# LN ahead of K, and Q units inside the K stage: a change of schedule in a fused attention and GEGLU kernel

## The chip, the cores and the metric

The kernel runs on one core of a Trainium2 chip. The metric is the device time of one execution in microseconds (us). Most executions of one kernel agree within a few tenths of a per cent; the widest spread of a kernel's fast runs here is 0.9%. A verdict of "faster" or "slower" needs more than 2%, and is "unclear" where the interval reaches that limit. PE is the engine of matmuls, PEld its weight loads, DVE the vector engine, ACT the scalar engine, POOL the GpSimd engine, SP the one that issues the DMAs here. The clock is the share of PE's full clock that the profile says was granted. LN is the layer norm; its last step on DVE is the normalise. K(n) and Gram(n) are the K and the Gram matmuls of tile n. PSUM is the memory that matmuls write to, in eight banks. A row-tiled pair is two Q units whose matmuls use 64 rows each and run side by side.

## The reference

All in bfloat16, S = 2048 tokens, D = 576, 32 heads of 18, F = 4608:

```python
xn  = layernorm(x)                                  # no gain, no bias
q, k, v = split(xn @ wqkv)                          # 32 heads of 18
phi = lambda t: where(t > 0, t + 1, exp(t)) + 1e-6
kv  = einsum("bhsd,bhse->bhde", phi(k), v);  z = sum_s phi(k)
o   = einsum("bhqd,bhde->bhqe", phi(q), kv) / (phi(q) . z + 1e-6)
out = x + o @ wo + (gelu(xn @ w_gate) * (xn @ w_up)) @ w_down
```

The kernel never forms V: it accumulates Gram = xn^T phi(k) over the tokens (with a column of ones for z), and kv is w_v^T Gram.

## The kernel before

The kernel writes its instructions in an order that it sorts out of planned times. Each engine works through its own instructions in that order, and semaphores hold it where an input or a buffer isn't ready. Only the first sixth of the span concerns us, up to the start of the gate/up matmuls:

- start: LN and PE transposes of tiles 0 to 3;
- K stage: for each of 16 tiles of 128 tokens LN on DVE and ACT, a crossbar transpose (a DMA) from tile 4 on, ten K matmuls, phi(k) on ACT, DVE and POOL, ten Gram matmuls;
- rest: 20 units of Q (4 chunks of 512 tokens by 5 groups of heads), the last part of Gram ("Gram B"), z and kv.

```python
def k_relu(n, hf):                     # one half of K, one PSUM bank
    if hf == 0:
        k_ea[n] = phi_tiles()          # e: 3 buffers, a: 2 buffers
    nc.scalar.activation(out=k_ea[n][0][:, hs], in_=ps_all[:, k_bank(n, hf), :HALF], func=ACT.Relu, scale=-1.0)
def k_max(n, hf):    ...               # DVE: a = max(ps, 0) + eps, same bank
def k_exp(n):        ...               # ACT: e = exp(-e)
def k_add(n):        ...               # POOL: pk = e + a
...
TILE = 2.5                             # planned us per tile
STEPS = [
    (lambda n: ln_half(n, 0), [3.02, 3.99, 6.44, 7.41, 9.44]),
    ...
    (ln_norm, [4.96, 5.69, 8.38, 10.77, 12.80]),
    (ln_dup, [5.43, 6.16, 8.85, 11.24, 13.27]),        # the transpose follows it
    ...
    (lambda n: k_half(n, 0), [6.86, 8.09, 10.30, 13.01, 15.56]),
    ...
]
...
for i in range(2, 2 * NCH):            # after the K stage: Q units 2 to 9, Gram B and copies between
    q_unit(i) ...
for k, items in enumerate([[(2, 0), (2, 1)], [(2, 2), (2, 3)], ...]):   # ten units in row-tiled pairs
    ...
```

A Q unit has one of two forms of phi. The add form is relu (ACT), max (DVE), exp (ACT), add (POOL). The min form is exp (ACT), max (DVE) and a `scalar_tensor_tensor` with min (DVE), which I call the min op.

## Time and profile before

| | before |
|---|---|
| time, median (in brackets the medians of the later rounds) | 538.54 (538.4 to 539.0) us |
| PE busy | 97% of the span of 537.7 us |
| K(4) starts | 17.21 us |
| first row-tiled Q pair starts | 75.50 us |
| gate/up starts | 85.77 us |
| stall in gate/up | 0.86 us at 91.82 |

In the table of waits, each line tells which engine and line stood still for whose result: total us, times, longest. The line that matters for the stretch from 5 to 62 us is:

```profile
PE ps_all L247 <- DMA xnT<-xn: 10.1, 9, 2.4
```

L247 is K, `xnT<-xn` the crossbar transpose. PE waits ten microseconds for transposes, and a clock that drops to half after one such wait, from 35.30 to 38.71 us, adds more. The prediction shows the other lines.

### The profile page before, as it was taken

How to read it: one execution, taken by the hardware profiler on the slowest of the kernel's cores; microseconds unless marked ns; L12 is line 12 of the kernel's file. 1: busy time of each engine (PE TensorE's matmuls, PEld its weight loads, DVE VectorE, ACT ScalarE, POOL GpSimd, SP SyncE). 2: the span in 40 equal slices, each digit the busy share in tenths (PEclk: the TensorE clock that was granted, in tenths of full speed). 3: DMA queues.
4: the chain of work that ended last, by engine and by line, in shares of the span. 5: the costliest groups of instructions: out<-in, count | busy, mean ns of one | idle time of the engine just before them, and what ended most of it. 6: DMA issues, size and time to landing. Idle time of an engine off the chain costs nothing.

```text
span 537.7 us, 10777 instructions
## 1 busy us (share of the span) xinstructions
PE 520.0 (97%) x4537; PEld 313.9 (58%) x4537; DVE 250.7 (47%) x414; ACT 143.7 (27%) x278; POOL 70.5 (13%) x85
## 2 busy tenths in 40 slices
PE   8778999999999999999999999999999999999997
PEld 7556676544457774444477754444677644445775
DVE  7745557687636813333358423333386133333100
...
PEclk9989999999999999999999999999999999999999
...
GB/s 226 154 132 154 40 1 45 237 249 271 217 131 12 12 11 166 155 152 158 146 33 24 12 121 154 155 145 159 77 11 23 78 155 153 156 134 2 12 12 23
DMA packets 106955, 57.90 MB, mean 108 GB/s; under 512 B 13402, under 2 KB 106522, under 8 KB 106906
## 3 DMA queue, kind: packets, MB, share of 16 engines
...
q14 instruction: 14, 0.11, 0.1%
...
## 4 chain that ended last, share of the span: by engine, by line
PE 86%; DMA 4%; DVE 3%; ACT 2%; POOL 1%; issue 1%; SPq 1%; DVEq 0%; ACTq 0%; POOLq 0%
PE ps_all L329 52%; PE ps_all L633 26%; PE ps_all L638 4%; DMA xnT<-xn 3%; PE ps_all L247 1%; PE ps_all L294 1%; POOL pqT L386 1%; PE ps_all L357 1%; DMA x_sb<-in_A_x_dram 1%; PE ps_all L442 1%; ACT phi_e L264 1%; DVE phi_a L384 1%; DVE phi_a L390 1%; DVE stats L210 1%; DVE phi_a L268 0%
## 5 line engine op out<-in xcount | busy, mean ns | idle before, releaser
L329 PE MATMUL ps_all<-xnT,wg 64*128 64x512 bf16 x1152 | 272.7, 376 | 0.0
L329 PE MATMUL ps_all<-xnT,wu 64*128 64x512 bf16 x1152 | 268.5, 376 | 0.0
L604 DVE TENSOR_TENSOR hT<-ps_all,gl 128x512 bf16<-128x512 f32 x144 | 99.4, 691 | 160.0 <-ACT gl L603 159.5
L603 ACT ACTIVATE gl<-ps_all 128x512 f32<-128x512 f32 x144 | 86.0, 598 | 312.5 <-PE ps_all L329 293.1
L329 PEld LDWEIGHTS <-wg 64*128 64x128 bf16 x1152 | 108.2, 94 | 68.9 <-issue 1.1
L633 PE MATMUL ps_all<-wd_sb,hT 128*128 128x288 bf16 x1152 | 147.0, 286 | 0.0
L329 PEld LDWEIGHTS <-wu 64*128 64x128 bf16 x1152 | 107.0, 94 | 67.2
L633 PEld LDWEIGHTS <-hT 128*128 128x128 bf16 x1152 | 112.3, 98 | 30.6 <-issue 1.3
L466 DVE RECIPROCAL den_sb<-den_sb 126x128 f32<-126x128 f32 (+1 forms) x80 | 68.3, 911 | 0.5
L469 POOL TENSOR_TENSOR pqT<-pqT,den_sb 126x512 bf16<-126x512 bf16 (+3 forms) x25 | 24.1, 966 | 297.7 <-DVE den_sb L466 279.1
L329 PE MATMUL ps_all<-xnT,wr 64*128 64x512 bf16 x288 | 61.9, 376 | 0.7 <-DVE phi_a L390 0.7
L641 DVE TENSOR_TENSOR res<-ps_all,x_sb 128x288 bf16<-128x288 f32 x32 | 14.6, 458 | 88.0 <-PE ps_all L638 88.0
L247 PE MATMUL ps_all<-wqkv_sb,xnT 128*128 128x288 bf16 x160 | 24.3, 296 | 10.8 <-DMA xnT<-xn 10.1
L329 PEld LDWEIGHTS <-wr 64*128 64x128 bf16 x288 | 17.1, 94 | 17.1 <-issue 0.7
L247 PEld LDWEIGHTS <-xnT 128*128 128x128 bf16 x160 | 14.9, 100 | 17.5 <-DMA xnT<-xn 12.1
L638 PE MATMUL ps_all<-m_sb,pqT 126*128 126x288 bf16 (+1 forms) x160 | 24.9, 285 | 0.0
L294 PE MATMUL ps_all<-hT,xn 128*128 128x288 bf16 (+3 forms) x192 | 23.4, 269 | 0.1
L279 POOL TENSOR_TENSOR hT<-phi_e,phi_a 128x576 bf16<-128x576 f32 x16 | 22.4, 1401 | 3.1 <-DVE phi_a L268 2.3
L268 DVE TENSOR_SCALAR phi_a<-ps_all 128x288 f32<-128x288 f32 x32 | 14.2, 450 | 17.5 <-ACT phi_e L264 15.8
L294 PEld LDWEIGHTS <-xn 128*128 128x128 bf16 (+1 forms) x192 | 18.5, 103 | 4.7 <-issue 0.6
L386 POOL TENSOR_TENSOR pqT<-phi_e,phi_a 126x512 bf16<-126x512 f32 (+1 forms) x13 | 16.3, 1267 | 21.2 <-DVE phi_a L384 17.3
L638 PEld LDWEIGHTS <-pqT 126*128 126x128 bf16 (+1 forms) x160 | 15.5, 97 | 4.1
...
## 6 DMA issues: line engine op xcount, KB each, us to landing
...
```

What stands on the lines that cost most here:

```text
L247: nc.tensor.matmul(ps_all[:, k_bank(n, hf), :HALF], lhsT=xnT[:, kt, n * P:(n + 1) * P], rhs=wqkv_sb[:, kt, D + hf * HALF:D + (hf + 1) * HALF],
L279: nc.gpsimd.tensor_tensor(out=pk[:, n, :], in0=e[:], in1=a[:], op=ALU.add)
L294: nc.tensor.matmul(ps_all[:m, b, col:col + w], lhsT=xn[:, n, j0:j0 + m], rhs=pk[:, n, d0:d0 + w], start=(n == 0 and col == 0), stop=(n == ...
L329: return nc.tensor.matmul(self.outs[i], lhsT=self.lhs(i, rows, kt), rhs=self.rhs(i, rows, kt), start=start, stop=stop, skip_group_check=True,)
L386: nc.gpsimd.tensor_tensor(out=pqT[:rows, c, cs], in0=e, in1=a, op=ALU.add)
L466: nc.vector.reciprocal(out=d[:, h:h + P], in_=d[:, h:h + P])
L469: nc.gpsimd.tensor_tensor(out=pqT[:rows, c, cols], in0=pqT[:rows, c, cols], in1=d, op=ALU.mult)
L603: nc.scalar.activation(out=gl[:], in_=ps_all[:, b[0], :], func=ACT.Gelu_apprx_tanh)
L604: nc.vector.tensor_tensor(out=hT[:, GUB * k + i, :], in0=ps_all[:, b[1], :], in1=gl[:], op=ALU.mult)
L633: nc.tensor.matmul(acc, lhsT=hT[:, f, j * P:(j + 1) * P], rhs=wd_sb[:, f, hs], start=(f == 0), stop=False,)
L638: nc.tensor.matmul(acc, lhsT=pqT[:rows, c, ts_], rhs=m_sb[:rows, c, hs], start=False, stop=(c == NCH - 1),)
L641: nc.vector.tensor_tensor(out=res[:, hs], in0=acc, in1=x_sb[:, n, hs], op=ALU.add)
```

## The change

Its intent: LN and the transpose behind it run further ahead of K (in the plan the transpose is issued 4.2 us before its K instead of 2.3), so that it has landed when K wants it, and the PE time that the K stage leaves is filled with Q. Twelve Q units go into the K stage, one per tile from tile 4 on. The last eight run as four row-tiled pairs right after it, ahead of Gram B, z and kv. K's relu and max cover both banks in one instruction from tile 4 on. The planned pace is 3.34 us per tile. The loads of w_q and of x are issued at once. The core of the diff:

```diff
+    load_w(0)
+    load_x(8, 4)
+    load_x(12, 4)
...
-        a = awork.tile([P, D], F32, name="phi_a", tag="phi_a", bufs=2)
+        a = awork.tile([P, D], F32, name="phi_a", tag="phi_a", bufs=3)
...
+        if hf is None:
+            e, a = (t[:].rearrange("p (h d) -> p h d", h=2) for t in k_ea[n])
+            return ps_all[:, k_bank(n, 0):k_bank(n, 0) + 2, :HALF], e, a
...
-    TILE = 2.5
+    TILE = 3.34
...
+        (ln_norm, [x_, 6.71, 7.42, 9.93, 11.02, 15.50, 16.52]),
+        (ln_dup, [5.86, 7.18, 7.89, 11.49, 11.73, 15.97, 18.87]),
+        (dma_transposes, [x_, x_, x_, x_, 12.02, 16.26, 19.16]),
+        (lambda n: k_half(n, 0), [6.85, 8.62, 11.23, 14.97, 16.67, 20.01, 23.33]),
...
+    Q_STEPS = [
+        (q_unit, [17.90, 21.23, 25.60, 28.93]),
+        (q_first, [19.29, 23.06, 26.80, 30.13]),
+        (q_max, [19.96, 24.03, 27.47, 30.80]),
+        (q_exp, [19.96, 23.73, 27.47, 30.80]),
+        (q_last, [21.20, 24.78, 28.22, 31.55]),
+    ]
+    NQ = 12
...
+    q_banks = _Ring([5, 6, 7, 0, 1, 2, 3, 4])
+    for k, units in enumerate([[12, 13], [15, 16], [17, 18], [14, 19], None]):
...
+    for n in range(NS):
+        g_accumulate(n, G_B)
```

More of the change, by code (lines that the diff above doesn't have):

```diff
@@ L39 @@
 NWARM = 38
-GLAG = 2
 TD = 4
@@ L148 @@
     kvT = persist.tile([P, NCH, CR], BF16, name="kvT")
+    nc.vector.memset(pqT[HP:P, NCH - 1, 0:2 * SC], 0.0)
+    nc.vector.memset(zrep[HP:P, NCH - 1, :], 0.0)
     def load_wo():
@@ L217, in ln_rstd, with ln_norm @@
         nc.scalar.activation(out=r, in_=r, func=ACT.Exp, scale=-0.5)
-    def ln_norm(n):
+    def ln_norm(n, c0=0, c1=D):
         nc.vector.tensor_scalar(
-            out=xn[:, n, 0:D], in0=x_sb[:, n, :], scalar1=mv[:, n, 0:1], scalar2=rstd[:, n:n + 1],
+            out=xn[:, n, c0:c1], in0=x_sb[:, n, c0:c1], scalar1=mv[:, n, 0:1], scalar2=rstd[:, n:n + 1],
             op0=ALU.subtract, op1=ALU.mult,
@@ L226, in ln_dup, with tp_bank, transposes, tp_copy @@
         (nc.gpsimd if n else nc.vector).tensor_copy(out=xn[:, n, D:640], in_=xn[:, n, 512:D])
-    tp_bank = ps_all[:, 7, :].bitcast(BF16).rearrange("p (k t) -> p k t", t=P)
-    def transposes(n):
-        for kt in range(KT):
-            nc.tensor.transpose(tp_bank[:, kt, :], xn[:, n, kt * P:(kt + 1) * P], ident[:])
+    vcopy, acopy = nc.vector.tensor_copy, nc.scalar.copy
+    def tp_bank(b):
+        return ps_all[:, b, :].bitcast(BF16).rearrange("p (k t) -> p k t", t=P)
+    def transposes(n, k0=0, k1=KT, b=7):
+        for kt in range(k0, k1):
+            nc.tensor.transpose(tp_bank(b)[:, kt, :], xn[:, n, kt * P:(kt + 1) * P], ident[:])
+    def tp_copy(n, k0=0, k1=KT, b=7, copy=acopy):
+        copy(out=xnT[:, k0:k1, n * P:(n + 1) * P], in_=tp_bank(b)[:, k0:k1, :])
     def dma_transposes(n):
         nc.sync.dma_start_transpose(xnT[:, :, n * P:(n + 1) * P], xn[:, n, 0:640])
-    def tp_copy(n):
-        copy = acopy if n else vcopy
-        copy(out=xnT[:, :, n * P:(n + 1) * P], in_=tp_bank[:, 0:KT, :])
     def k_bank(n, hf):
@@ L254, in phi_tiles, with k_part, k_relu, k_max @@
         e = awork.tile([P, D], F32, name="phi_e", tag="phi_e", bufs=3)
-        a = awork.tile([P, D], F32, name="phi_a", tag="phi_a", bufs=2)
+        a = awork.tile([P, D], F32, name="phi_a", tag="phi_a", bufs=3)
         return e, a
     k_ea = {}
-    def k_relu(n, hf):
-        if hf == 0:
+    def k_part(n, hf):
+        if n not in k_ea:
             k_ea[n] = phi_tiles()
+        if hf is None:
+            e, a = (t[:].rearrange("p (h d) -> p h d", h=2) for t in k_ea[n])
+            return ps_all[:, k_bank(n, 0):k_bank(n, 0) + 2, :HALF], e, a
         hs = slice(hf * HALF, (hf + 1) * HALF)
-        nc.scalar.activation(out=k_ea[n][0][:, hs], in_=ps_all[:, k_bank(n, hf), :HALF], func=ACT.Relu, scale=-1.0)
-    def k_max(n, hf):
-        hs = slice(hf * HALF, (hf + 1) * HALF)
-        nc.vector.tensor_scalar(
-            out=k_ea[n][1][:, hs], in0=ps_all[:, k_bank(n, hf), :HALF],
-            scalar1=0.0, scalar2=EPS_ATT, op0=ALU.max, op1=ALU.add,
-        )
+        return ps_all[:, k_bank(n, hf), :HALF], k_ea[n][0][:, hs], k_ea[n][1][:, hs]
+    def k_relu(n, hf=None):
+        ps, e, _ = k_part(n, hf)
+        nc.scalar.activation(out=e, in_=ps, func=ACT.Relu, scale=-1.0)
+    def k_max(n, hf=None):
+        ps, _, a = k_part(n, hf)
+        nc.vector.tensor_scalar(out=a, in0=ps, scalar1=0.0, scalar2=EPS_ATT, op0=ALU.max, op1=ALU.add)
     def k_exp(n):
@@ L278, in k_add @@
         e, a = k_ea.pop(n)
-        nc.gpsimd.tensor_tensor(out=pk[:, n, :], in0=e[:], in1=a[:], op=ALU.add)
+        (nc.gpsimd if n < NS - 1 else nc.vector).tensor_tensor(out=pk[:, n, :], in0=e[:], in1=a[:], op=ALU.add)
     G_A = {
@@ L287 @@
     }
-    G_B = {3: [(0, 0, 0, 288), (1, 0, 288, 288)]}
+    G_B = {3: [(5, 0, 0, 288), (6, 0, 288, 288)]}
     def g_accumulate(n, pieces):
@@ L297, in g_accumulate @@
                 )
-    G_B_AT = {5: range(2), 6: range(2, 9), 7: range(9, 16)}
-    vcopy, acopy = nc.vector.tensor_copy, nc.scalar.copy
     G_COPIES = {
-        4: [(0, G_A, 0, acopy), (0, G_A, 1, vcopy), (2, G_A, 0, acopy), (2, G_A, 1, vcopy)],
-        5: [(1, G_A, 0, acopy), (2, G_A, 2, vcopy)],
-        6: [(4, G_A, 2, acopy), (1, G_A, 1, vcopy)],
-        7: [(4, G_A, 0, acopy), (4, G_A, 1, vcopy), (3, G_B, 0, acopy), (3, G_B, 1, vcopy)],
-        99: [(3, G_B, 0, acopy), (3, G_B, 1, vcopy)],
+        0: [(0, 0, acopy), (2, 0, vcopy), (0, 1, acopy), (2, 1, vcopy)],
+        1: [(1, 0, acopy), (2, 2, vcopy), (4, 2, acopy), (1, 1, vcopy), (4, 0, acopy), (4, 1, vcopy)],
     }
@@ L315 @@
     SYNC = mybir.DependencyInfo(mybir.DependencyClass.Sync, mybir.DependencyReason.DATA)
-    banks = _Ring([2, 3, 4, 5, 6, 7, 0, 1])
+    banks = _Ring([3, 4, 5, 6, 7, 0, 1, 2])
     class _Unit:
@@ L349 @@
     q_banks = _Ring([7])
+    q_out, q_ea = {}, {}
+    MIN_UNITS = (2, 5, 8, 11, 13, 14, 16, 18)
     def q_unit(i):
@@ L360, in q_unit @@
             )
-        q_phi(i, sc, c, ps)
-    def q_pair(items):
-        rows = DH * HCH[items[0][1]]
-        b = [q_banks.next(), q_banks.next()]
-        outs = [ps_all[:rows, b_, :] for b_ in b]
-        def lhs(i, r, kt):
-            q0 = DH * HOFF[items[i][1]]
-            if kt == 4 and r.start:
-                return wq_lo[r, q0:q0 + rows]
-            return wqkv_sb[r, kt, q0:q0 + rows]
-        return _Unit(outs, lhs, lambda i, r, kt: xnT[r, kt, items[i][0] * SC:(items[i][0] + 1) * SC], nc.sync)
@@ L377, in q_phi, with q_pair, lhs, rhs @@
-    def q_phi(i, sc, c, ps):
-        rows = DH * HCH[c]
-        cs = slice(sc * SC, (sc + 1) * SC)
-        e, a = phi_tiles()
-        e, a = e[:rows, :SC], a[:rows, :SC]
-        if i % 3 != 2:
+        q_out[i] = ps
+    def q_pair(units):
+        rows = DH * HCH[units[0] % NCH]
+        for i in units:
+            q_out[i] = ps_all[:rows, q_banks.next(), :]
+        def lhs(a, r, kt):
+            q0 = DH * HOFF[units[a] % NCH]
+            if kt == 4 and r.start == 0:
+                return wqkv_sb[r, kt, q0:q0 + rows]
+            return (wq_lo if kt == 4 else wqkv_sb[:, kt])[r, q0:q0 + rows]
+        def rhs(a, r, kt):
+            sc = units[a] // NCH
+            return xnT[r, kt, sc * SC:(sc + 1) * SC]
+        return _Unit([q_out[i] for i in units], lhs, rhs, nc.sync)
@@ L383, in q_phi, with q_at, q_first @@
+    def q_at(i):
+        sc, c = divmod(i, NCH)
+        rows = DH * HCH[c]
+        if i not in q_ea:
+            q_ea[i] = [t[:rows, :SC] for t in phi_tiles()]
+        return (*q_ea[i], q_out[i], pqT[:rows, c, sc * SC:(sc + 1) * SC])
+    def q_first(i):
+        e, _, ps, _ = q_at(i)
+        if i not in MIN_UNITS:
             nc.scalar.activation(out=e, in_=ps, func=ACT.Relu, scale=-1.0)
-            nc.vector.tensor_scalar(out=a, in0=ps, scalar1=0.0, scalar2=EPS_ATT, op0=ALU.max, op1=ALU.add)
@@ L385, in q_phi, with q_max @@
-            nc.scalar.activation(out=e, in_=e, func=ACT.Exp, scale=-1.0)
-            nc.gpsimd.tensor_tensor(out=pqT[:rows, c, cs], in0=e, in1=a, op=ALU.add)
         else:
             nc.scalar.activation(out=e, in_=ps, func=ACT.Exp)
-            nc.vector.tensor_scalar(out=a, in0=ps, scalar1=0.0, scalar2=1.0 + EPS_ATT, op0=ALU.max, op1=ALU.add)
-            nc.vector.scalar_tensor_tensor(
-                out=pqT[:rows, c, cs], in0=e, scalar=EPS_ATT, in1=a, op0=ALU.add, op1=ALU.min)
+    def q_max(i):
+        _, a, ps, _ = q_at(i)
+        one = 0.0 if i not in MIN_UNITS else 1.0
+        nc.vector.tensor_scalar(out=a, in0=ps, scalar1=0.0, scalar2=one + EPS_ATT, op0=ALU.max, op1=ALU.add)
@@ L394, in mask_pair, with q_exp, q_last @@
+    def q_exp(i):
+        e, _, _, _ = q_at(i)
+        if i not in MIN_UNITS:
+            nc.scalar.activation(out=e, in_=e, func=ACT.Exp, scale=-1.0)
+    def q_last(i):
+        e, a, _, out_ = q_at(i)
+        if i not in MIN_UNITS:
+            nc.gpsimd.tensor_tensor(out=out_, in0=e, in1=a, op=ALU.add)
+        else:
+            nc.vector.scalar_tensor_tensor(out=out_, in0=e, scalar=EPS_ATT, in1=a, op0=ALU.add, op1=ALU.min)
     def mask_pair(dst, b4, b1):
@@ L420, in kv_stage @@
         b4, b1 = q_banks.next(), q_banks.next()
-        for c in range(NCH):
-            rows = DH * HCH[c]
-            for kt in range(KT):
+        for kt in (0, 1, 2, 4, 3):
+            for c in range(NCH):
+                rows = DH * HCH[c]
                 nc.tensor.matmul(
@@ L426, in kv_stage @@
                     rhs=g_sb[:, kt, c * CR:c * CR + rows],
-                    start=(kt == 0 and c in (0, 4)), stop=(kt == KT - 1), skip_group_check=True,
+                    start=(kt == 0 and c in (0, 4)), stop=(kt == 3), skip_group_check=True,
                 )
@@ L470, in den_norm @@
         return scale
-    TILE = 2.5
+    TILE = 3.34
+    x_ = None
     STEPS = [
-        (lambda n: ln_half(n, 0), [3.02, 3.99, 6.44, 7.41, 9.44]),
-        (lambda n: ln_half(n, 1), [3.51, 4.48, 6.93, 7.90, 9.93]),
-        (ln_rstd, [4.14, 5.11, 7.56, 10.12, 11.84]),
-        (ln_norm, [4.96, 5.69, 8.38, 10.77, 12.80]),
-        (ln_dup, [5.43, 6.16, 8.85, 11.24, 13.27]),
-        (transposes, [5.66, 6.57, 9.14, 11.53, 13.62]),
-        (tp_copy, [6.07, 6.98, 9.56, 12.27, 14.12]),
-        (lambda n: k_half(n, 0), [6.86, 8.09, 10.30, 13.01, 15.56]),
-        (lambda n: k_half(n, 1), [7.47, 9.43, 10.91, 13.91, 16.46]),
-        (lambda n: k_relu(n, 0), [7.99, 9.28, 11.56, 13.84, 16.55]),
-        (lambda n: k_relu(n, 1), [8.27, 10.55, 12.83, 15.11, 17.39]),
-        (lambda n: k_max(n, 0), [8.72, 10.41, 12.44, 14.61, 17.27]),
-        (lambda n: k_max(n, 1), [9.08, 11.11, 13.28, 15.60, 17.84]),
-        (k_exp, [8.73, 11.12, 13.29, 15.61, 18.10]),
-        (k_add, [9.59, 11.73, 14.01, 16.29, 19.88]),
-    ]
@@ L493 @@
-    SPIN = [(5.67, 7), (6.58, 2), (7.48, 3), (8.10, 2), (9.15, 3)]
-    G_AT = [11.82, 14.53, 17.07, 19.62, 22.16]
-    def at(times, n):
-        return times[n] if n < len(times) else times[-1] + TILE * (n - len(times) + 1)
-    todo = [(at(times, n), step, n) for n in range(NS) for step, times in STEPS
-            if n < TD or step not in (transposes, tp_copy)]
-    todo += [(at(STEPS[4][1], n) + 0.01, dma_transposes, n) for n in range(TD, NS)]
-    loads = [(7.0, lambda n: load_x(8, 4)), (9.5, lambda n: load_x(12, 4))]
@@ L504 @@
-    loads += [(13.5, lambda n: load_w(0)), (18.5, lambda n: load_w(2)), (23.5, lambda n: load_wo())]
-    loads += [(26.0 + 2.5 * i, lambda n, i=i: load_gu(i // 2, i % 2)) for i in range(2 * NWBUF)]
-    todo += [(t, step, 0) for t, step in loads]
-    todo += [(at(G_AT, n), lambda n: g_accumulate(n, G_A), n) for n in range(NS - GLAG)]
-    todo += [(at(STEPS[7][1], NS - 1) - 0.01, q_unit, 0), (at(G_AT, NS - GLAG) - 0.01, q_unit, 1)]
-    todo += [(at(STEPS[-1][1], 4 + n) + 0.01, lambda n: nc.gpsimd.memset(pqT[HP:P, NCH - 1, n * SC:(n + 1) * SC], 0.0), n)
-             for n in range(2)]
@@ L513 @@
-    todo += [(at(STEPS[-1][1], 7) + 0.01, lambda n: nc.gpsimd.memset(zrep[HP:P, NCH - 1, :], 0.0), 0)]
-    todo += [(t, spin, count) for t, count in SPIN]
+        (lambda n: ln_half(n, 0), [3.02, 3.99, 5.20, 7.05, 8.60, 12.08, 13.38]),
+        (lambda n: ln_half(n, 1), [3.51, 4.48, 5.96, 7.76, 9.09, 13.81, 14.53]),
+        (ln_rstd, [4.14, 6.05, 6.59, 8.44, 10.44, 14.44, 15.94]),
+        (ln_norm, [x_, 6.71, 7.42, 9.93, 11.02, 15.50, 16.52]),
+        (ln_dup, [5.86, 7.18, 7.89, 11.49, 11.73, 15.97, 18.87]),
@@ new lines @@
+        (transposes, [x_, 7.47, 9.23, 11.85]),
+        (tp_copy, [x_, 7.88, 9.88, 12.44]),
+        (dma_transposes, [x_, x_, x_, x_, 12.02, 16.26, 19.16]),
+        (lambda n: k_half(n, 0), [6.85, 8.62, 11.23, 14.97, 16.67, 20.01, 23.33]),
+        (lambda n: k_half(n, 1), [7.76, 9.52, 10.62, 13.33, 16.68, 20.02, 23.34]),
+        (lambda n: k_relu(n, 0), [7.58, 11.15, 13.00, 15.70]),
+        (lambda n: k_relu(n, 1), [8.87, 10.87, 12.16, 14.06]),
+        (k_relu, [x_, x_, x_, x_, 18.01, 21.35, 24.67]),
@@ new lines @@
+        (lambda n: k_max(n, 0), [8.24, 11.72, 13.45, 16.15]),
+        (lambda n: k_max(n, 1), [9.57, 11.36, 12.82, 14.66]),
+        (k_max, [x_, x_, x_, x_, 18.73, 22.23, 25.39]),
+        (k_exp, [9.32, 11.60, 13.45, 16.16, 18.73, 22.07, 25.39]),
+        (k_add, [10.08, 12.33, 14.18, 16.88, 19.54, 23.04, 26.20]),
+        (lambda n: g_accumulate(n, G_A), [12.14, 13.94, 15.64, 18.98, 22.31, 24.57, 27.89]),
+    ]
+    Q_STEPS = [
[5 more added lines that the diff above has]
+    ]
@@ new lines, with timed @@
+    NQ = 12
+    def timed(steps, count):
+        for step, times in steps:
+            for n in range(count):
+                last = len(times) - 1
+                if n < last or len(times) > 4 or steps is Q_STEPS:
+                    t = times[min(n, last)]
+                    if t is not None:
+                        yield t + TILE * max(n - last, 0), step, n
+                elif n == last:
+                    yield times[n], step, n
+    todo = [*timed(STEPS, NS), *timed(Q_STEPS, NQ)]
@@ new lines @@
+    todo += [
+        (4.96, lambda n: ln_norm(n, 0, 3 * P), 0), (5.57, lambda n: ln_norm(n, 3 * P, D), 0),
+        (5.33, lambda n: transposes(n, 0, 3, 7), 0), (6.09, lambda n: transposes(n, 3, KT, 4), 0),
+        (5.63, lambda n: tp_copy(n, 0, 3, 7, acopy), 0), (6.44, lambda n: tp_copy(n, 3, KT, 4, vcopy), 0),
+    ]
+    todo += [(t, spin, count) for t, count in [(5.70, 3), (6.10, 5), (7.40, 3), (8.30, 3), (9.40, 4)]]
+    loads = [lambda n: load_w(2), lambda n: load_wo()]
+    loads += [lambda n, i=i: load_gu(i // 2, i % 2) for i in range(2 * NWBUF)]
@@ L516 @@
+    todo += [(19.2 + TILE * i, step, 0) for i, step in enumerate(loads)]
     for _, step, n in sorted(todo, key=lambda x: x[0]):
@@ L523, in g_copy @@
         copy(out=g_sb[:m, kt, d0:d0 + w], in_=ps_all[:m, b, col:col + w])
-    q_banks = _Ring([5, 6, 7])
-    for i in range(2, 2 * NCH):
-        if i == 7:
-            q_banks = _Ring([2, 3, 4, 5, 6, 7])
-        q_unit(i)
-        if 3 <= i < 3 + GLAG:
-            g_accumulate(NS - GLAG + i - 3, G_A)
-        for n in G_B_AT.get(i, ()):
-            g_accumulate(n, G_B)
-        for kt, pieces, part, copy in G_COPIES.get(i, ()):
-            g_copy(kt, pieces, part, copy)
-        if i == 8:
-            z_stage()
-        if i == 8:
-            kv_stage()
-    q_banks = _Ring(list(range(8)))
+    q_banks = _Ring([5, 6, 7, 0, 1, 2, 3, 4])
     prev = None
-    for k, items in enumerate([[(2, 0), (2, 1)], [(2, 2), (2, 3)], [(2, 4), (3, 4)], [(3, 0), (3, 1)], [(3, 2), (3, 3)], None]):
-        if items:
-            u = q_pair(items)
+    for k, units in enumerate([[12, 13], [15, 16], [17, 18], [14, 19], None]):
+        if units:
+            u = q_pair(units)
             u.p1()
+        for kt, part, copy in G_COPIES.get(k, ()):
+            g_copy(kt, G_A, part, copy)
         if prev:
             prev[1].p2()
-            for i, (sc, c) in enumerate(prev[0]):
-                q_phi(2 * k + i, sc, c, prev[1].outs[i])
-        prev = (items, u)
+            for step in (q_first, q_max, q_exp, q_last):
+                for i in prev[0]:
+                    step(i)
+        prev = (units, u)
+    for n in range(NS):
+        g_accumulate(n, G_B)
+    g_copy(3, G_B, 0, acopy)
+    g_copy(3, G_B, 1, vcopy)
+    q_banks = _Ring([7, 0, 1, 2])
+    z_stage()
+    kv_stage()
     scales = []
```

## The prediction

> **What bounds the kernel now.** I read the page first: PE is busy 97% of the span, so only the stretches where it is not can give anything. The slices say where these lie: in the first sixth. I then cut that sixth into four stretches with the table of busy time by stretch (start:end, length, then busy us and instruction count of PE, PEld, DVE, ACT and POOL, clock, DMA share, GB/s).
>
> ```profile
> PE   8778999999999999999999999999999999999997
> PEclk9989999999999999999999999999999999999999
> ```
>
> ```profile
> 17.20:55.40 38.20, 28.68 (x226) 21.64 (x226) 20.31 (x59) 19.50 (x53) 19.15 (x24) 0.96 0.73 155
> 55.40:75.50 20.10, 19.95 (x148) 14.10 (x149) 11.88 (x21) 11.89 (x25) 10.29 (x8) 1.00 0.08 19
> 75.50:91.82 16.32, 15.26 (x138) 11.50 (x138) 10.72 (x19) 12.00 (x20) 8.30 (x7) 1.00 0.04 12
> ```
>
> The K stage (17.2 to 55.4) leaves PE idle for 9.5 us; Q and Gram after it and the paired Q units lose some 1.2 us. The chain of waits says why (start, length, what):
>
> ```profile
> 23.83 0.30 DVE xn L220
> ...
> 24.26 0.25 POOL xn L226
> ...
> 24.52 3.56 DMA xnT<-xn
> 28.07 0.05 issue
> 28.12 0.80 PE ps_all L247 x5
> ...
> 29.52 0.46 DVE phi_a L268
> 29.98 0.38 DVE stats L210
> ...
> 31.21 4.25 DMA xnT<-xn
> ```
>
> It is a ring: K of tile n releases a max on DVE; behind it in DVE's order stands the LN of tile n+2; its crossbar transpose takes 3.6 to 4.3 us here (2.6 where no 648 KB weight load is ahead); then K of n+2. So about 6.8 us per two tiles, while PE has only K and Gram to do. The timeline of PE shows the price and one more loss, ten K matmuls in 2.58 instead of 1.40 us after a long wait, at a granted clock of 0.50 in that half microsecond.
>
> ```profile
> 35.51 2.58 PE L247 MATMUL ps_all<-wqkv_sb,xnT 128*128 128x288 bf16 x10 [2.45 <-DMA xnT<-xn]
> 42.16 1.40 PE L247 MATMUL ps_all<-wqkv_sb,xnT 128*128 128x288 bf16 x10 [0.51 <-DMA xnT<-xn]
> 91.82 0.37 PE L329 MATMUL ps_all<-xnT,wr 64*128 64x512 bf16 x1 [0.71 <-DVE phi_a L390]
> ```
>
> Gate/up starts at 85.77 us and stalls once, 0.86 us of pace at 91.82, since the Q nonlinearities still run on DVE until 92.8. From there to the end PE is full and the change touches nothing.
>
> **What the Trainium skill says.** (1) "SBUF — State Buffer", Who interferes with whom: DVE in a 2-port mode, or with two SBUF inputs, and GpSimd take one shared port pair as an exclusive lock; who comes first keeps it for the whole instruction. The trace agrees to the hundredth: the min op of a Q unit takes 0.69 us alone and ends 0.55 after POOL's add ends when they meet.
>
> ```profile
> 61.73 1.41 POOL L279 TENSOR_TENSOR hT<-phi_e,phi_a 128x576 bf16<-128x576 f32 x1
> 62.53 1.16 DVE L391 SCALAR_TENSOR_TENSOR pqT<-phi_e,phi_a 126x512 bf16<-126x512 f32 x1
> 66.90 0.69 DVE L391 SCALAR_TENSOR_TENSOR pqT<-phi_e,phi_a 126x512 bf16<-126x512 f32 x1
> ```
>
> 62.53+1.16 = 63.69 = 63.14+0.55. The LN normalise (0.38 alone) does the same: the two met by POOL's add end 0.17 after it. (2) "PSUM — Partial Sum Buffer", PSUM bank collisions raise a hardware error: two engines must not access one bank at once, reads included. In the trace DVE's max starts 0.10 after ACT's relu of the same bank ends, always. The new relu and max over both banks therefore run one after the other. (3) "TensorE: Matmul & The Clock Gate", Back-to-back issue gap: N/2.4+2.5 ns when warm, 122.5 ns for N=288; 14 Gram matmuls start within 1.72 us, 123 ns each.
>
> **The change, part by part.** PE's work, from starts to starts: K 10 x 0.124 = 1.24; Gram A 0.98 per tile; a Q unit 1.08; a row-tiled pair 1.94 (81.08 to 83.02), 0.97 per unit. Twelve single units instead of ten cost 2 x 0.11 = 0.2 us more. Everything else of PE only moves. A tile of the K stage with a Q unit is 1.24+0.98+1.08 = 3.30 us of PE, which is why the plan has 3.34: PE is to be full, and the lead of the transpose in the plan is 23.33-19.16 = 4.2 us.
>
> Start. x(3) still lands at 8.2, x(4..7) at 9.6 (issue 4.4 plus 5.2). DVE reaches max(0,1) near 11.3 instead of 9.6 as planned; POOL's add of tile 0 stands ahead of the copy for tile 3, and the transposes of tile 3 come at 13.2 instead of 11.85. Through G(0), K(3), G(1), G(2), with the lock once, K(4) starts at about 17.9; it is 17.21 now.
>
> A steady tile, counted from the start of K(n), with durations of the trace (576 wide estimated from the 288 and 512 wide: relu 0.66, max 0.76): relu 1.50 to 2.16, max 2.26 to 3.02, POOL add 3.16 to 4.56, so Gram(n) can start at 4.64. PE wants it at 1.24+0.98+1.08+1.24 = 4.54. Balanced to 0.1 us. Then what stands in between: the normalise of n+3 is ready at 3.3, finds POOL's add holding the lock and ends at 4.73 instead of 3.7; statistics, the Q max (0.69), statistics and aggregate (0.6) follow, so max(n+1), ready at 5.56, starts at 6.2 to 6.3; in a tile whose Q unit uses the min form, after another 0.61, at 6.9. It holds both K banks: K(n+2), due at 6.60, waits for 7.0 to 7.6, and Gram(n+1) some 0.3 to 0.4 more. After such a slip the next tile is free of it. I carried this order by hand from tile 4 to 15, with 3.7 us for the transposes behind the two 648 KB loads (K(7) waits 0.4, and this replaces another stall) and 2.7 to 3.2 for the rest (no wait; their lead is 3.3 or more). Starts of K(4) to K(15), relative: 0, 3.3, 7.0, 11.0, 14.7, 18.5, 21.8, 25.7, 29.0, 32.5, 36.0, 39.3: 3.58 us per tile. Gram(15), its add on DVE behind POOL's lock, ends at 44.2. So the K stage ends at 17.9+44.2 = 62.1, planned 59 (57.95 plus 0.98, rounded).
>
> Rest. Four pairs 4 x 1.94 = 7.76; Gram B 32 x 0.123 = 3.94; z 0.26 and kv 1.34 (72.72, 72.98, 74.32 now). For PE alone gate/up starts at 62.1+13.3 = 75.4. But every pair but the last has an add unit, then a min unit: POOL's add starts about 1.85 after the pair's matmuls, just before the min op wants the lock, and the min op ends 0.55 after it. DVE then needs about 2.55 us per pair against 1.94. Starting 65.2 it ends near 75.8, then copies Gram B (0.45), then the last kv matmuls: gate/up at about 76.5, 1.1 later.
>
> Sum: gate/up moves from 85.77 to 76.5, 9.3 us; the stall of 0.86 at 91.82 goes, since the Q nonlinearities end before gate/up and the gelu table load (1.28 at 90.28) is hidden. 10.2 us, 538.5-10.2 = 528.3. The DVE memsets at 2 us lie in 1.1 us of its idle time: free. The third buffer for the max tile removes waits for POOL of 1.4 us: inside the above.
>
> **Rivals.** (a) The plan holds: no lock stalls, gate/up at 59.1+13.3 = 72.4, gain 14.2, 524.3. For it: PE's work does fit, and the lead of transposes is real; against it: DVE and POOL were held by the lock in six instructions already. (b) Transposes stay the bound: the copy of the duplicate columns stands behind a Q add on POOL, which shortens the lead from 4.2 to about 3.3 us, while one transpose in the profile took 4.6. If every loaded transpose lands at 4.2 or more, each such tile waits about 0.9, eight tiles 7 us less what the slips give back: 532 to 533. (c) The nonlinearities bound: ACT 3.0, DVE up to 3.3, POOL 2.9 per 3.30 us; if waits between them add 0.3 more per tile, 12 x 0.3 = 3.6 us: about 532. My number is a mild form of (c).
>
> **Range and chances.** Two per cent is 10.8 us, 527.8; my gain is 10.2. The sum rests on some twenty places where two engines meet within 0.2 us; I give it 1.5 to 2 us either way, somewhat more on the slow side: 525.2 to 531.5. So 0.44 for faster by over 2%, 0.54 for within, 0.02 for slower; only broken ordering could lose ten microseconds.
>
> **What would show it.** Right: PE's timeline has K, Gram, Q in turn at about 3.6 us per tile, no clock below 1.0 after 10 us, waits of K on DVE's max and of Gram on POOL's add rather than on the transposes, except near tile 7; normalise and min ops of 1.0 us and more ending 0.17 and 0.55 after a POOL add; Gram(15) ends near 62, gate/up starts near 76.5 and no stall after it. Wrong: K waiting on xnT from DMA in most tiles (rival b), a pace of 3.35 and gate/up before 73.5 (rival a), gate/up waiting again for its banks, or a different pace after gate/up begins, which I hold to be untouched.

## The result, and the profile after

The changed kernel takes 531.18 us (530.84 to 532.26, 4 runs), the kernel before 538.96 us (538.05 to 539.46) in the same rounds. The ratio is 0.9861 with an interval of 0.984 to 0.9882: 7.8 us or 1.4% less. Ratios here and below are the mean time of one kernel's fast runs over that of the other's of the same rounds, so not quite the ratio of the medians quoted.

The slices of the page answer to those shown of before:

```profile
PE   7999999999999999999999999999999999999997
PEclk9999999999999999999999999999999999999999
```

PE is busy from the second slice on, no slice shows a clock below 90%, and its mean is 0.999. The stretches (same columns as in the prediction: K(4) to the first pair, then up to gate/up) are:

```profile
18.71:64.02 45.31, 42.33 (x310) 30.98 (x310) 36.04 (x65) 32.44 (x64) 29.18 (x30) 1.00 0.53 122
64.02:78.43 14.41, 13.78 (x136) 9.55 (x135) 12.52 (x20) 9.47 (x19) 4.92 (x4) 1.00 0.00 1
```

The K stage now holds twelve Q units and leaves PE idle for 3 us instead of 9.5. What PE still waits for from 18 to 80 us, in the table of waits, is hardly a transpose any more. In the last line stand PE's weight loads, which do wait for one:

```profile
PE ps_all L254 <- DVE phi_a L283: 1.2, 2, 0.6
PE ps_all L306 <- POOL hT L291: 0.8, 4, 0.2
PE ps_all L366 <- DVE phi_a L409: 0.6, 1, 0.6
PE ps_all L454 <- DVE g_sb L569: 0.6, 1, 0.6
PE ps_all L306 <- DVE hT L291: 0.4, 1, 0.4
...
PEld L254 <- DMA xnT<-xn: 1.0, 1, 1.0
```

L254 is K, L283 its max, L306 Gram, L291 the add of K, L366 a Q unit, L409 its max, L454 kv and L569 the copies of Gram. The table puts a wait down to what came last, and one of the two waits for the max hides a transpose. Before K(8), at 33.55, the max ended at 33.50, and the weight load that the transpose had held until then started at 33.47. So without the max K(8) would have started less than 0.1 us earlier. That transpose took 4.8 us to land, behind a big load; in all ten profiles with the lead and Q inside the K stage, K(8) waited 0.4 to 1.0 us for its transpose, in two of them for the max at the same time. The other wait, at 45.06, is the max's own. How it comes about is seen in the timeline of all engines (start, length, engine, line, what; in brackets the idle time before and who ended it):

```profile
40.45 0.24 POOL L231 COPY xn<-xn 128x64 bf16<-128x64 bf16 x1
40.51 1.71 DVE L225 TENSOR_SCALAR xn<-x_sb,mv,rstd 128x576 bf16<-128x576 bf16 x1 [0.19 <-ACT rstd L222]
40.64 1.40 POOL L291 TENSOR_TENSOR hT<-phi_e,phi_a 128x576 bf16<-128x576 f32 x1
...
42.50 0.67 DVE L409 TENSOR_SCALAR phi_a<-ps_all 126x512 f32<-126x512 f32 x1
...
43.70 0.64 DVE L421 SCALAR_TENSOR_TENSOR pqT<-phi_e,phi_a 126x512 bf16<-126x512 f32 x1
...
44.25 0.75 DVE L283 TENSOR_SCALAR phi_a<-ps_all 128x576 f32<-128x576 f32 x1
...
45.06 1.39 PE L254 MATMUL ps_all<-wqkv_sb,xnT 128*128 128x288 bf16 x10 [0.59 <-DVE phi_a L283]
45.15 1.46 POOL L291 TENSOR_TENSOR hT<-phi_e,phi_a 128x576 bf16<-128x576 f32 x1 [2.63 <-ACT phi_e L402]
...
46.67 1.15 PE L306 MATMUL ps_all<-hT,xn 128*128 128x288 bf16 x10 [0.22 <-POOL hT L291]
```

The normalise (L225) takes 1.71 us instead of about 0.42. POOL's add ends at 42.04, and the normalise ends just under 0.2 later, at 42.22. It started 0.13 us before that add, but POOL's small copy (L231) was running, and when the copy ended the add went ahead of the waiting normalise. From 42.13 on DVE works without a pause up to the max of K (L283), which is late by the whole hold, so K waits 0.59 us for its banks and Gram 0.22 for the add. This is the lock that the prediction took from the Trainium skill, "SBUF — State Buffer", Who interferes with whom. Five of the nine normalises from 20 us on were held in this way (1.33 to 1.71 us).

The paired stage shows the same on DVE, in the min ops (L421) and the Gram copy behind them, and on PE in what waits for that copy:

```profile
69.31 1.54 DVE L421 SCALAR_TENSOR_TENSOR pqT<-phi_e,phi_a 126x512 bf16<-126x512 f32 x1
...
72.08 1.33 DVE L421 SCALAR_TENSOR_TENSOR pqT<-phi_e,phi_a 126x512 bf16<-126x512 f32 x1
...
77.10 0.67 DVE L421 SCALAR_TENSOR_TENSOR pqT<-phi_e,phi_a 72x512 bf16<-72x512 f32 x1
77.70 0.44 DVE L569 CAST g_sb<-ps_all 128x288 bf16<-128x288 f32 x1
```

```profile
78.19 0.30 PE L454 MATMUL ps_all<-g_sb,wqkv_sb 128*126 128x126 bf16 x3 [0.63 <-DVE g_sb L569]
78.43 0.39 PE L336 MATMUL ps_all<-xnT,wr 64*128 64x512 bf16 x2
```

Gate/up starts at 78.43, 7.34 us earlier than before. From 100 us on the trace shows no wait of PE at all, and the stall at 91.82 has no counterpart.

### The profile page after: what moved, and what is told of

Read it like the earlier page. It is cut to its first block, busy times and chain, and to the rows that moved or that the text cites. A ratio compares the mean times of both kernels' runs of the same rounds, so it can differ in the third digit from the quotient of the medians.

```text
span 529.3 us, 10714 instructions
## 1 busy us (share of the span) xinstructions
PE 518.7 (98%) x4530; PEld 315.1 (60%) x4530; DVE 257.5 (49%) x407; ACT 142.9 (27%) x266; POOL 66.7 (13%) x80
## 4 chain that ended last, share of the span: by engine, by line
PE 88%; DVE 5%; ACT 3%; POOL 1%; DMA 1%; issue 0%; SPq 0%; ACTq 0%; POOLq 0%; DVEq 0%
PE ps_all L336 54%; PE ps_all L675 27%; PE ps_all L680 4%; DVE phi_a L409 1%; PE ps_all L306 1%; DVE xn L225 1%; DVE pqT L421 1%; PE ps_all L254 1%; POOL hT L291 1%; DMA x_sb<-in_A_x_dram 1%; ACT phi_e L279 1%; PE ps_all L366 1%; ACT phi_e L287 1%; DVE stats L215 1%; PE ps_all L472 1%; DVE phi_a L283 1%
## 5 line engine op out<-in xcount | busy, mean ns | idle before, releaser
L336 PE MATMUL ps_all<-xnT,wu 64*128 64x512 bf16 x1152 | 271.7, 376 | 0.0
L336 PEld LDWEIGHTS <-wu 64*128 64x128 bf16 x1152 | 108.3, 94 | 66.2
L336 PE MATMUL ps_all<-xnT,wr 64*128 64x512 bf16 x288 | 55.1, 376 | 0.0
L336 PEld LDWEIGHTS <-wr 64*128 64x128 bf16 x288 | 14.5, 94 | 16.8 <-issue 0.7
L254 PE MATMUL ps_all<-wqkv_sb,xnT 128*128 128x288 bf16 x160 | 22.9, 286 | 1.4 <-DVE phi_a L283 1.2
L306 PE MATMUL ps_all<-hT,xn 128*128 128x288 bf16 (+3 forms) x192 | 22.4, 266 | 1.6 <-POOL hT L291 0.8
L291 POOL TENSOR_TENSOR hT<-phi_e,phi_a 128x576 bf16<-128x576 f32 x15 | 21.5, 1434 | 13.5 <-DVE phi_a L283 7.3
L306 PEld LDWEIGHTS <-xn 128*128 128x128 bf16 (+1 forms) x192 | 18.1, 101 | 6.5 <-issue 3.1
L254 PEld LDWEIGHTS <-xnT 128*128 128x128 bf16 x160 | 15.0, 98 | 7.5 <-issue 1.1
L409 DVE TENSOR_SCALAR phi_a<-ps_all 126x512 f32<-126x512 f32 (+1 forms) x20 | 13.3, 678 | 5.2 <-ACT phi_e L402 4.8
```

Of the source, the lines that this page charges most:

```text
L254: nc.tensor.matmul(ps_all[:, k_bank(n, hf), :HALF], lhsT=xnT[:, kt, n * P:(n + 1) * P], rhs=wqkv_sb[:, kt, D + hf * HALF:D + (hf + 1) * HALF],
L291: (nc.gpsimd if n < NS - 1 else nc.vector).tensor_tensor(out=pk[:, n, :], in0=e[:], in1=a[:], op=ALU.add)
L306: nc.tensor.matmul(ps_all[:m, b, col:col + w], lhsT=xn[:, n, j0:j0 + m], rhs=pk[:, n, d0:d0 + w], start=(n == 0 and col == 0), stop=(n == ...
L336: return nc.tensor.matmul(self.outs[i], lhsT=self.lhs(i, rows, kt), rhs=self.rhs(i, rows, kt), start=start, stop=stop, skip_group_check=True,)
L409: nc.vector.tensor_scalar(out=a, in0=ps, scalar1=0.0, scalar2=one + EPS_ATT, op0=ALU.max, op1=ALU.add)
```

## The experiments

All gave a correct result. "Start" is the time at which gate/up starts in the profile, "K part" the time from K(4) to the first row-tiled Q pair. The K part of the six runs that share its code (the changed kernel, e2, e5, e9, e10, e13) lies between 44.4 and 45.7 us, 45.0 in the mean.

| run | time, us | ratio to before | K part, us | start, us |
|---|---|---|---|---|
| changed kernel | 531.18 | 0.9861 | 45.3 | 78.43 |
| e1_norm_late | 529.42 | 0.9829 | 43.3 | 76.66 |
| e2_min_first | 533.74 | 0.9897 | 44.4 | 79.93 |
| e3_lead_undone | 543.43 | 1.0089 | 55.8 | 91.54 |
| e4_q_after | 543.58 | 1.0088 | 53.6 | 92.06 |
| e5_start_order | 531.29 | 0.9856 | 44.6 | 78.14 |
| e9_bufs4 | 531.30 | 0.9859 | 45.7 | 78.93 |
| e10_bufs4_min_first | 530.40 | 0.9847 | 45.3 | 77.68 |
| e11_three | 528.85 | 0.982 | 43.3 | 76.53 |
| e13_norm4_late | 531.08 | 0.9863 | 44.9 | 78.18 |
| e14_four | 529.62 | 0.9831 | 43.3 | 75.53 |
| e15_four_nomin | 529.07 | 0.9823 | 42.9 | 76.37 |

**Control, e0_after.** No edit.

> The changed kernel as it is, as the control on this chip. Both theories: 531.2 us, ratio to the kernel before 0.986; gate/up starts at 78.4 us, K(4) at 18.7, ten or so normalise ops of tiles 4 to 12 with half of them 1.33 us or longer.

Three executions took 530.89 to 531.50 us, ratio 0.9862: the first result holds on this chip. The fourth, the profiled one, took 1111.43 us. It is left out. Its trace shows PE at about half pace from beginning to end (the ten matmuls of K(5) take 2.58 us up to the start of the next, not 1.22), while DVE's normalises take their usual 0.43 and 1.33 us. The trace holds no clock record at all, so the "clock 1.0" of this run is not a reading. Why PE ran so is open. The profile of the first result stands for the changed kernel.

**The lead undone, e3_lead_undone.** The LN of tiles 7 to 15 goes back by one tile; each list of LN times gets one entry more:

```diff
-        (ln_norm, [x_, 6.71, 7.42, 9.93, 11.02, 15.50, 16.52]),
+        (ln_norm, [x_, 6.71, 7.42, 9.93, 11.02, 15.50, 16.52, 23.20]),
-        (dma_transposes, [x_, x_, x_, x_, 12.02, 16.26, 19.16]),
+        (dma_transposes, [x_, x_, x_, x_, 12.02, 16.26, 19.16, 25.84]),
```

> The LN of tiles 7 to 15 with its copy and its transpose goes back by one tile (3.34 in the plan), Q units stay in the K stage. Theory (the lead is what takes the transposes off the path; Q alone does not): normalise of n+2 stands behind the max of n, at 3.3 to 4.7 us after K(n) starts, its copy behind POOL's Q add at 6.3, its transpose lands at 9.2 to 10.5, so K(n+2) waits for xnT each time: 4.6 to 5.2 us per tile instead of 3.65, gate/up 9 to 14 us later, 540 to 545 us, slower than the kernel before. Rival (the lead is small change; filling PE with Q is the gain): within 2 us of 531.

It took 543.43 us (2 runs), 0.9% more than the kernel before. The table of waits of PE has the transposes back, and in the timeline the first of these waits cost the clock as well:

```profile
PE ps_all L254 <- DMA xnT<-xn: 11.0, 7, 3.1
```

```profile
34.64 2.58 PE L254 MATMUL ps_all<-wqkv_sb,xnT 128*128 128x288 bf16 x10 [3.12 <-DMA xnT<-xn]
```

The theory held, time and mechanism, though not "each time": seven of the nine moved tiles waited. By the time one tile of lead decides 12 us. The trace gives 10.5 us for the K part; K(4) also started 2.6 us later in this execution, before the moved tiles: the five matmuls of K(0) took 1.20 us up to the next instead of 0.81, and a full clock is recorded only from 14.1 us on. Against the kernel before the interval of the ratio, 1.0064 to 1.0114, lies above 1.

**Q after the K stage, e4_q_after.** The lead stays, all Q times move by 45 us:

```diff
-    q_banks = _Ring([7])
+    q_banks = _Ring([5, 6, 7])
-        (q_unit, [17.90, 21.23, 25.60, 28.93]),
+        (q_unit, [62.90, 66.23, 70.60, 73.93]),
```

> The LN lead stays, but the twelve Q units run after Gram A of tile 15 (banks 5, 6 and 7 in turn) instead of inside the K stage. Theory (lead and Q each do half: the lead takes the transposes off, and Q fills the PE time that the ring K, max, LN, transpose still leaves): K stage without Q at 2.5 to 2.8 us per tile, 12 tiles some 31 us, then twelve Q units that ACT (0.60+0.63 each) holds at 1.2 to 1.3 us, 15 us; K(4) to the first paired unit about 47 instead of 45.3, time 532 to 534. Rival A (the lead alone is the gain): 531 or less. Rival B (Q inside is most of it): 538 or more.

It took 543.58 us, well beyond my theory's 532 to 534: rival B is right, Q has to be inside. The timeline of PE shows where I was wrong:

```profile
23.03 1.39 PE L254 MATMUL ps_all<-wqkv_sb,xnT 128*128 128x288 bf16 x10
24.57 1.15 PE L306 MATMUL ps_all<-hT,xn 128*128 128x288 bf16 x10 [0.16 <-POOL hT L291]
26.33 1.39 PE L254 MATMUL ps_all<-wqkv_sb,xnT 128*128 128x288 bf16 x10 [0.62 <-DVE phi_a L283]
```

K tiles start every 2.96 to 3.31 us, not every 2.5 to 2.8. The relu and the max over both banks must end before the next K can write them, and that is some 3.0 us after K starts (K(4) 20.05, relu 21.53 to 22.18, max 22.21 to 22.97, K(5) 23.03). With Q in the tile PE needs 3.30 us anyway, and this hold is covered; without Q it sets the pace in most tiles (six waits, 3.0 us in all; two more, 1.1 us, were for a transpose). Eleven such intervals took 34.3 us, twelve Q units 14.4 us more, and the pairs ran partly at half clock (77.22 to 80.63) after a wait of 1.59 us for a Gram copy. So the two halves of the change need each other: either alone is some 12 us slower than both together, and 0.9% slower than the kernel before. But the hold comes with the third part of the change, K's relu and max over both banks. That part was not undone by itself, so e4 does not show what the lead alone gives with one bank per instruction.

**The normalise behind the Q max, e1_norm_late.** The transposes keep their place; only the order on DVE changes, so that POOL's add has ended when the normalise comes:

```diff
-        (ln_norm, [x_, 6.71, 7.42, 9.93, 11.02, 15.50, 16.52]),
+        (ln_norm, [x_, 6.71, 7.42, 9.93, 11.02, 15.50, 16.52, 19.97, 24.04, 27.48]),
```

> The LN normalise of tiles 7 to 15 is put behind the Q max on DVE, where POOL's K add has ended; nothing else moves. Lock theory (the normalise held by POOL's add delays the Q max, the statistics and the next tile's max, which holds both K banks): normalise ops at most 0.45 us, the waits of K for DVE's max (0.60 at 33.55 and 0.59 at 45.06) shrink or go, K(4) to the start of the paired Q units falls from 45.3 to about 43 us and the time from 531.2 to 528.5 to 529.5. Rival (the chain K, relu, max, add, Gram itself sets the pace, about 3.35 plus the min ops; the held normalise lies beside it): under 0.5 us of change. Second rival (the later normalise makes the crossbar transposes late): K waits for xnT, slower.

It took 529.42 us against 531.35 in the same rounds. The lines of the normalise between 18 and 60 us (count, then shortest, median and longest in ns), of the changed kernel and of this one:

```profile
L225 DVE TENSOR_SCALAR xn<-x_sb,mv,rstd x10: 423/882/1705, 18.6 to 52.0; 128x576 bf16<-128x576 bf16 x10
```

```profile
L225 DVE TENSOR_SCALAR xn<-x_sb,mv,rstd x10: 418/424/466, 18.8 to 52.0; 128x576 bf16<-128x576 bf16 x10
```

The same ten instructions are 882 and 424 ns in the median; the work is the same and the neighbour is not. The waits of K for DVE's max are gone; at K(8) one for its transpose stays, 0.51 us. The K part fell from 45.3 to 43.3 us as the lock theory said, 1.7 us below the mean of the six runs with the old order. The new order takes away one thing more: DVE's own waits for `rstd` from ACT in front of the normalise, 2.1 us in six places. The trace of the changed kernel tells the two apart where PE waited. At 24.01 (a Q unit, 0.63 us) and at 45.06 (K, 0.59 us) the normalise before had been held 0.92 and 1.29 us beyond its 0.42, but had waited only 0.38 and 0.19 us for `rstd`, so the lock alone is long enough.

**Min first in the pairs, e2_min_first.**

```diff
-    for k, units in enumerate([[12, 13], [15, 16], [17, 18], [14, 19], None]):
+    for k, units in enumerate([[13, 12], [16, 15], [18, 17], [14, 19], None]):
```

> In the first three row-tiled pairs the min unit comes ahead of the add unit, as in the fourth pair already. Lock theory: the min ops of these pairs take 0.69 us instead of 1.33 to 1.54, DVE reaches the last Gram B copy before it is ready, the wait of 0.63 at 78.19 goes: gate/up 0.7 us earlier, time 530.2 to 530.7. Rival (DVE is behind because of the PSUM copies and the ACT-before-DVE order of each bank, not the lock): wait stays, no change.

Both missed: it was slower, 533.74 us. The min ops did fall to 0.68 us. But now POOL's add comes second and lasts 1.58 us, and ACT waits for it, as its timeline shows; then kv waits for both Gram copies, and the 3.4 us after it (80.50 to 83.92) run at half clock (same columns as the stretches above, clock third from the end):

```profile
71.19 0.60 ACT L402 ACTIVATE phi_e<-ps_all 126x512 f32<-126x512 f32 x1 [1.20 <-POOL pqT L419]
```

```profile
78.95 0.27 PE L454 MATMUL ps_all<-g_sb,wqkv_sb 128*126 128x126 bf16 x2 [1.36 <-ACT g_sb L569]
79.69 0.30 PE L454 MATMUL ps_all<-g_sb,wqkv_sb 128*126 128x126 bf16 x3 [0.47 <-DVE g_sb L569]
```

```profile
82.00:83.00 1.00, 1.00 (x8) 0.40 (x6) 0.00 (x0) 0.00 (x0) 0.00 (x0) 0.50 0.00 0
```

From the first pair to gate/up it took 15.7 us instead of 14.4, and from gate/up to the end 452.6 instead of 450.9, which is the clock. The four executions spread from 531.54 us (mean clock 1.000) to 534.66 (0.995), so the second part does not come every time.

ACT waits for POOL because three pairs of work tiles go round, so a unit needs the tile of one of the pair before. That made a second theory: two limits, the lock and the three work tiles. The next two runs tell them apart.

**Own work tiles, e9_bufs4, and both, e10_bufs4_min_first.** The paired units get four pairs of tiles in a free part of the hT buffer; e10 has the order of e2 as well:

```diff
-            q_ea[i] = [t[:rows, :SC] for t in phi_tiles()]
+            if i < NQ:
+                q_ea[i] = [t[:rows, :SC] for t in phi_tiles()]
+            else:
+                c0 = NS * D + 4 * SC * (len(q_ea) % 4)
+                q_ea[i] = [h_store[:rows, s0:s0 + 2 * SC].bitcast(F32) for s0 in (c0, c0 + 2 * SC)]
```

> The eight paired Q units get four pairs of work tiles of their own (in the part of the hT buffer that Gram does not use) instead of sharing three; their order stays. Lock theory (in each pair DVE's min op waits for POOL's add, 2.56 us per pair): ACT's waits for POOL go, the min ops stay at 1.33 us, the wait of 0.63 before the last kv matmuls stays, time 531.2 plus or minus 0.4. Rival (three work tiles are the limit of the paired stage): the wait goes, 0.6 us faster.

> The four pairs of own work tiles together with the min unit first in each pair. With min first and three work tiles the stage ran at 3.08 us per pair, ACT waiting 1.2 to 1.34 us for POOL's add of the pair before. Theory (two limits, either of which binds alone: the lock, and the three work tiles): with both off, DVE needs about 1.9 us per pair, PE's 1.94 binds, the wait before the last kv matmuls goes, gate/up starts 0.6 us earlier than in the changed kernel at the same Gram end, time 530.4 to 530.8. Rival (the min op put first takes the port pair from POOL, whose add then lasts 1.58 us and ends too late whatever the tiles): the wait stays, 531.5 or more.

Tiles alone change nothing: 531.30 us, the min ops still 1.32 to 1.55 us, the wait of kv still 0.6. Both together gave 530.40 us: min ops of 0.68 us, one pair every 1.94 us on DVE, and no wait before the last kv matmuls. From the first pair to gate/up it took 13.6 us (64.06 to 77.68) instead of 14.4, which all six profiles with the old order agree on (14.35 to 14.41). The two limits are shown. With the add unit first the lock binds and hides the tiles, with the min unit first the tiles bind. The single time differs from the control by about its spread, so the verdict rests on the 0.8 us of the stretch.

**The start, e5_start_order and e13_norm4_late.** The statistics of tile 2 behind tile 0's work; the normalise of tile 4 behind two maxes:

```diff
-        (lambda n: ln_half(n, 0), [3.02, 3.99, 5.20, 7.05, 8.60, 12.08, 13.38]),
+        (lambda n: ln_half(n, 0), [3.02, 3.99, 6.45, 7.05, 8.60, 12.08, 13.38]),
-        (lambda n: ln_half(n, 1), [3.51, 4.48, 5.96, 7.76, 9.09, 13.81, 14.53]),
+        (lambda n: ln_half(n, 1), [3.51, 4.48, 6.46, 7.76, 9.09, 13.81, 14.53]),
```

```diff
-        (ln_norm, [x_, 6.71, 7.42, 9.93, 11.02, 15.50, 16.52]),
+        (ln_norm, [x_, 6.71, 7.42, 9.93, 11.725, 15.50, 16.52]),
```

> The statistics of tile 2 go behind the two halves of tile 0's normalise and its PSUM copy on DVE, so that DVE does not stand waiting for x of tile 2 (1.23 us until 6.55) with tile 0 unfinished; nothing else moves. Theory (that wait is what made the start late by 0.8 us against the prediction): K(0) starts near 6.9 instead of 7.86 and K(4) at 17.9 to 18.3 instead of 18.71, time 530.5 to 531. Rival (x of tile 3 and the later order set K(4), the early time is lost again): K(0) earlier, K(4) within 0.2 us of 18.7, no change of the time.

> Only the normalise of tile 4 moves, behind the two maxes of tile 1 on DVE, so that POOL's add of tile 0 no longer holds it (and these maxes behind it) until 13.58. Theory (the late start of K(4), 18.7 instead of the predicted 17.9, is the same lock, met once in the start): Gram of tile 0 starts at 13.5 to 13.8 instead of 14.36, K(4) at 17.9 to 18.3, time 530.4 to 530.9. Rival (K(4) waits for the transpose of tile 4, now issued some 0.3 us later, or for ACT): K(4) at 18.6 or later, no gain.

Neither moved the time (531.29 and 531.08 us). In e5 K(0) came at 6.57, but K(4) at 19.14:

```profile
6.57 0.97 PE L254 MATMUL ps_all<-wqkv_sb,xnT 128*128 128x288 bf16 x5
...
19.14 1.39 PE L254 MATMUL ps_all<-wqkv_sb,xnT 128*128 128x288 bf16 x10
```

In e13 Gram(0) came at 14.15, later than the 13.5 to 13.8 expected, and K(4) at 18.90. The start differs from one execution to the next: in seven profiles of runs that share the start up to tile 4 (the changed kernel, e1, e2, e3, e4, e9, e10) K(0) lies between 7.62 and 9.12, and K(4) between 18.71 and 21.35. A gain of half a microsecond can't be seen through that. A part of the spread can be read off. DVE waited 1.00 to 2.26 us for x of tile 2 in six of these runs, and PE then waited for the normalise of tile 0 behind it. After such a wait of PE of 1.91 us (e4), 1.62 (e11) and 1.72 (e15) the clock stood at 0.50 for 3.4 us, and K(4) came at 19.57 to 20.05; after 1.18 to 1.45 us (six profiles) it stayed at 1.00. The rival of e5 fits better (later steps set K(4)), but what sets it is not settled.

**Together: e11_three, e14_four, e15_four_nomin.** e11 is e1 with e10; e14 adds e13; e15 also has only one min unit in the K stage:

```diff
-    MIN_UNITS = (2, 5, 8, 11, 13, 14, 16, 18)
+    MIN_UNITS = (11, 13, 14, 16, 18)
```

> The late normalise of e1 with the own work tiles and min-first pairs of e10. If the lock in the K stage (1.9 us in e1) and that in the paired stage (0.8 us in e10) are separate terms, they add: 528.6 plus or minus 0.4, ratio to the kernel before near 0.9815, gate/up at about 76. Rival (the K stage's gain is given back in the paired stage, which then starts with more DVE work left): 529.2 or more.

> e11 with the normalise of tile 4 late as well: all three places of the lock removed. If e13's term is real and adds: 528.0 plus or minus 0.5, K(4) at about 18.2; if the start is given back: as e11.

> e14 with no min unit in the K stage but the last (units 2, 5 and 8 in the add form as well). If the min op's 0.61 us on DVE still delays the next tile's max and the K banks once the lock is gone: up to 1 us faster, 527.2 to 527.8. Rival (with the lock gone the min op lies in DVE's idle time, and three more adds of 1.27 us make POOL, at 2.9 of 3.30 us in every tile, late for its K adds): same as e14 or slower, Gram waiting for POOL.

e11 took 528.85 us (528.39 to 529.18, ratio 0.982, 0.9798 to 0.9842): 2.3 us less than the 531.18 of the changed kernel, which comes from other rounds. On the trace the two terms of the lock add: from K(4) to gate/up 2.0 us in e1, 0.8 in e10, 2.8 here. e14 took 529.62 (528.53 to 529.87) and e15 529.07 us (528.15 to 530.10). These three can't be told apart by time. By the trace, from K(4) to gate/up they took 57.0, 57.0 and 56.6 us, the changed kernel 59.7. So the min op in the K stage is worth at most some tenths once the lock is gone (with the lock left in, it was not tried), and the start is left as noise. All three beat both kernels. So does e1, whose edit is one line; e11's gain over e1 rests on the stretch of the trace. Against the kernel before e11 is 1.8% faster, which with its interval is "unclear" at the 2% limit, as is e15.

## Why the prediction was right

The time on record was 528.3 us with a range of 525.2 to 531.5; 531.18 is inside by 0.3 us (the slowest of its four executions, 532.26, is not, so there is some luck in it), and the most likely verdict was the one that came. The gain was 7.8 us where I had 10.2. By its own steps:

- **The bound before.** Right: PE's waits for transposes fell from 10.1 us to one of 1.0 on its weight loads, at K(8). e3 shows that it is the lead that does it.
- **Start, K(4) at 17.9.** Too early by 0.8 (18.71). DVE stood 1.23 us for x of tile 2 with tile 0 half done, which I had not seen in the new order. But e5, which takes this wait away, did not bring K(4) forward, so the cause of the 0.8 is open. It is more than the spread of the start: in no profile with the new start did K(4) come before 18.57.
- **K part, 44.2 us to the end of Gram(15).** It took 45.3, to 64.02. The starts of K(4) to K(15), relative, came as 0, 3.3, 7.4, 10.7, 14.8, 18.5, 21.8, 26.4, 30.0, 33.4, 36.8, 40.4. Up to K(10) no entry is off by more than 0.4; the rest is mostly the tile shown above, where the normalise lasted 1.71 us behind POOL's copy and K add. My count by hand had let the normalise in first there. I had also left out that the Q units have one bank (unit 1 waited 0.63 us for its predecessor's max, which a held normalise had made late), and the wait for a loaded transpose, 0.4 us at K(7) in my count, came at K(8) with 0.6.
- **The lock as the cause of the slips.** Right for the slips at 24.01 and 45.06, and shown by e1 with the reading of `rstd` above: 2.0 us of the K part (1.7 against the mean of its like). The slip of K(8) is the transpose's.
- **Rest, 14.4 us to gate/up with 1.1 for DVE.** It took 14.41. Here the sizes fitted and the reason was half the story: the lock does set the pace (e9), but turning the order round, which that story invites, fails because of the work tiles (e2). Only e10 gains.
- **Stall of 0.86 us in gate/up gone, nothing else touched.** Right.
- **Readings that were wrong.** The clock of 0.50 after the wait of 2.45 us lasted 3.4 us, not "that half microsecond", and slowed Gram too (ten matmuls in 1.56 instead of 1.15 us). The max does not "always" start 0.10 us after the relu of its bank: in the kernel before 18 of 52 did (0.09 to 0.11), the others 0.03 to 1.2 us after, and in the changed kernel the shortest gap is 0.03. Of the sums, 39.3 over 11 tiles is 3.57 and not 3.58, and the plan's end of the K stage is 58.9 where rival (a) has 59.1. None of these moves the result.

The terms on the trace give 7.34 + 0.86 = 8.2 us, the spans 537.7 - 529.3 = 8.4. The medians give 7.8, the difference being of the size of the runs' spread.

Of the rivals, (a) would have needed no lock; e15, without most of it, still takes 56.6 us from K(4) to gate/up, where (a), whose plan has K(4) at 16.67, needs 55.7. (b) came true for one tile of twelve: the transpose of K(8) took 4.8 us behind a big load. (c) was the right family, in the mild form.

## What to carry to other kernels

When work is packed onto DVE and POOL side by side, add to each DVE instruction that the lock can hold (here the normalise and the min op) the time until POOL's current instruction ends, and its next one too where POOL goes straight on, as at 40.51; the order on DVE decides whether it is paid, and moving one instruction can be worth more than removing one. A buffer hold or a ring of work tiles that costs nothing at one pace becomes the bound at another, so undo the halves of a change one by one before crediting either. Where a wait costs PE its clock, add that: 3.4 us at half clock after the kv waits of e2 cost 1.7 us. And ask of a wait what would have ended it next: here a transpose stood behind the max at K(8).

## What the Trainium skill lacked or had wrong

- "SBUF — State Buffer", Who interferes with whom: the lock showed in every normalise and min op that started while an add on POOL had most of its time to run, but the page gives no figure for what is left once the lock is free. Here the normalise ended 0.16 to 0.17 us after POOL's add, the min op 0.55 us after; and POOL's add behind a min op lasted 1.58 us instead of 1.27. Nor does it say who gets the pair when POOL goes straight from one instruction to the next: at 40.51 the normalise, there 0.13 us before the add, was passed over.
- "Advanced Engine Details and Errata", X-Bar Transpose (TRN2): it gives a bandwidth and no latency; "VectorE: DVE Perf Modes", The three transpose paths, has 1309 ns for 128x128, and no page that I found has a time for more, or beside other loads. The transposes of one 128x640 tile took 2.6 to 4.8 us from issue to landing in the changed kernel, up to 5.2 in e5, and about 1.2 us each on SP's queue (one 1.96); the latency is what sized the lead.
- "TensorE: Matmul & The Clock Gate", What's actually happening: its table has the clock fall after an idle window of about 3.4 us. Here it fell to 0.50, for 3.4 us each time, after single waits of 2.45 us (before), 3.12 us (e3) and 1.59 us (e4), and after two of 1.36 and 0.47 us with 0.27 us of matmuls between (e2). A wait of 2.62 us in e3 (at 45.67) left it at 1.00. So the length of one wait did not decide.
- No page that I read speaks of an execution in which PE keeps about half pace throughout and no clock is recorded: 1111.43 us once, in the control.
